# Splitting the last matmul tile of an attention-and-MLP kernel into two column halves, and storing two early tiles together

## The chip, the cores and the metric

The kernel runs on one core of a Trainium2 chip. A core has five engines with instruction streams of their own: TensorE (PE in the profile; its weight loads are listed as PEld), VectorE (DVE), ScalarE (ACT), GpSimd (POOL) and SyncE (SP), which here only issues transfers. Transfers are moved by 16 DMA engines. Data lives in SBUF (128 partitions); matmul results land in PSUM, which has banks of 512 fp32 columns per partition. The metric is the device time of one execution, in microseconds; lower is better.

## What is computed

```python
def attn(x, state):            # x [8,8,512,64], state [8,8,32,64], fp32
    scale = 1.0 / np.sqrt(64)
    a  = softmax(scale * x @ state^T)      # each token reads the state
    xread = a @ state
    a2 = softmax(scale * state @ x^T)      # the state reads the tokens
    sread = a2 @ x
    return concatenate([xread, sread], axis=2)      # 512 + 32 rows per batch

def reference(x, state, moe_w_in, moe_w_out):
    t = attn(x, state)                     # [8,8,544,64]
    t = t.transpose(0, 2, 1, 3).reshape(8 * 544, 512)
    h = t @ moe_w_in                       # [4352, 2048]
    return maximum(0.01 * h, h) @ moe_w_out  # [4352, 512] fp32
```

## The kernel before

The work is done batch by batch, b = 0 to 7, and the order of every engine's instructions is written out by hand. For one batch, `a_scores` makes the scores, the softmaxes run on DVE and ACT, and `a_m` folds the state into the first weight matrix (M = state times w_in), so that `ff1` makes one 128-row slice of the hidden layer from the softmax alone: 16 slices per batch, each evicted by ACT (L447) with the leaky ReLU. The second product (hidden layer times w_out, 512 token rows by 512 columns per batch) is spread between the slices of the next batch.

For batches 0 and 1 the second product is plain: `piece(b, hT, i, jq)` adds four of the sixteen contraction steps of the token tile i (0 to 3), with matmuls of 512 columns (L547). `y_store` (L554) copies the finished PSUM tile into SBUF and issues its store on SP (L558); tiles 2 and 3 of batch 0 are kept in one PSUM tile of two banks, `pyw`, and copied by ACT and DVE.

From batch 2 on the second product uses a scheme with seven block products in place of eight. `product(b, n, v)` (L615) makes product n for the half v of the rows: eight matmuls of 256 columns (L642) that add into PSUM "x" (n = 1, 6, 7, 4) or "b" (n = 2, 5, 3). Between them `keep` copies a partial sum away, and `y_add` adds a kept sum while evicting. For the last batch, 7, PSUM "x" is made of two separate places (`ppw`), one for each half v. Product 4 is the last to be added; what stands in "x" after it is the output block.

The order of the end is: a loop over c = 0, 1 that makes the hidden layer for all state rows (`f_product`, L520, matmuls of 128 columns) with batch 7's products 2, 5, 6 and 7 in between; the second product of the state rows (`two_product`, L699, `ppr`), whose results leave in eight stores (L1285), four on SP's queue and four on ACT's; product 3 of batch 7 with its eviction by DVE (L739) and its store (L745); and product 4:

```python
    for v in range(2):
        product(b, 4, v)
        (VEC, SCA)[v](y_block(b, 1, 0)[:, v], prods[b]["x"][v])
        nc.sync.dma_start(rows_of(b)[2 + v][:, :HN], y_block(b, 1, 0)[:, v])
```

`VEC` and `SCA` are copies on DVE and ACT. HN is 256.

At the start PE has little to do until the first inputs are in. `spin(p, n, w)` (L161) issues n matmuls of w columns on zeros, whose results nobody reads; they stand between the transposes `x0_t` (L784) and the scores `scores0` (L800) of batch 0's heads, and DVE takes maxima from the scores (`max0`, L830).

A buffer of a pool is written again when its last readers are done. Transfers that SP and ACT issue carry one of eight completion counters in turn, and a transfer waits for the one that used its counter before.

Of the kernel before, what the change touches and what calls it, by code (L numbers as in the profile page):

```python
# [9 lines left out]
P = 128  # L10
B, H, S, D = 8, 8, 512, 64
NS = 32
DFF = 2048
DM = 512
# [6 lines left out]
FP32 = mybir.dt.float32  # L21
AF = mybir.ActivationFunctionType
ALU = mybir.AluOpType
# [4 lines left out]
def kernel(  # L28
# [9 lines left out]
    nc = tc.nc  # L38

    consts = ctx.enter_context(tc.tile_pool(name="consts", bufs=1))  # L40
# [5 lines left out]
    ypool = ctx.enter_context(tc.tile_pool(name="ypool", bufs=3))  # L46
    psum = ctx.enter_context(tc.tile_pool(name="psum", bufs=2, space=bass.MemoryType.PSUM))
# [5 lines left out]
    VEC, SCA, POO = nc.vector.tensor_copy, nc.scalar.copy, nc.gpsimd.tensor_copy  # L53
# [104 lines left out]
    def spin_bank():  # L158
        return psum.tile([P, S], FP32, name="pspin", tag="py")

    def spin(p, n, w=S):  # L161
        for _ in range(n):
            nc.tensor.matmul(p[:, :w], lhsT=idle[:, :P], rhs=idle[:, :w], start=True, stop=True)
# [375 lines left out]
    ys = {}  # L539
# [12 lines left out]
            y_store(b, i, copy)  # L552

    def y_store(b, i, copy):  # L554
        tag = ("ysb", "s1", "ysb", "s6")[i]
        ysb = ypool.tile([P, DM], FP32, name="ysb", tag=tag, bufs=3 if tag == "ysb" else 1)
        copy(ysb[:], ys[b, i].py)
        nc.sync.dma_start(rows_of(b)[i], ysb[:])  # L558

    HN = DM // 2  # L560
    HJ = 8
# [12 lines left out]
    def w_block(r, c, j0, j1):  # L574
        return w_out_bf[:, HJ * r + j0:HJ * r + j1, HN * c:HN * (c + 1)]
# [12 lines left out]
    hTs, sums, prods = {}, {}, {}  # L588
# [20 lines left out]
    def w_of(n, j):  # L609
        if n < 4:  # L610
            r, c = {1: (0, 0), 2: (1, 0), 3: (1, 1)}[n]
            return w_block(r, c, j, j + 1)[:, 0]
        return tw[{4: 4, 5: 1, 6: 2, 7: 3}[n]][j // 4][:, j % 4]

    def product(b, n, v, j0=0, j1=8):  # L615
        q = prods.setdefault(b, {})
        bank = "x" if n in (1, 6, 7, 4) else "b"
        first = n in (1, 2, 5) and v == 0 and j0 == 0
        if first:
            if b == B - 1 and n == 1:  # L620
                ts = [psum.tile([P, 2, DM], FP32, name="ppw", tag=t, bufs=1) for t in ("sc", "big")]
                q[bank] = [t[:, 0, :HN] for t in ts]
                q["whole", bank] = None
            else:
                t = psum.tile([P, 2, HN], FP32, name=f"pp{bank}", tag="py")
                q[bank] = [t[:, u] for u in range(2)]
                q["whole", bank] = t[:]
        wide = b == B - 1 and n == 1
        q["open", bank] = first or (wide and j0 == 0)
        at = slice(P * v, P * (v + 1))  # L630
        low = slice(HN * 1 + P * v, HN * 1 + P * (v + 1))
        for j in range(j0, j1):
            lhsT = {
                1: lambda: hTs[b][:, j, at],
                2: lambda: hTs[b][:, HJ + j, at],
                4: lambda: hTs[b][:, HJ + j, low],
                3: lambda: sums[b, 4][:, j, at],
                5: lambda: sums[b, 1][:, j, at],
                6: lambda: sums[b, 2][:, j, at],
                7: lambda: sums[b, 3][:, j, at],  # L640
            }[n]()
            nc.tensor.matmul(  # L642
                q[bank][v], lhsT=lhsT, rhs=w_of(n, j), start=q["open", bank] and j == 0,
                stop=j == 7, skip_group_check=True,
            )

# [71 lines left out]
    def keep(b, n):  # L718
        q = prods[b]
        if n == 5:  # L720
            t = consts.tile([P, 2, HN], FP32, name="s5", tag="stf4")
        else:
            t = ypool.tile([P, 2, HN], FP32, name=f"s{n}", tag=f"s{n}", bufs=1)
        q[n] = t
        for to, of in bank_parts(q, "b" if n == 5 else "x", t[:]):
            SCA(to, of)

    def y_block(b, u, c):
        q = prods[b]
        if ("y", u) not in q:  # L730
            q["y", u] = ypool.tile([P, 2, DM], FP32, name="ysb", tag="ysb")
        return q["y", u][:, :, HN * c:HN * (c + 1)]

    def y_add(b, u, c, bank, n):
        q = prods[b]
        kept = q[n][:]
        for v, (to, of) in enumerate(bank_parts(q, bank, y_block(b, u, c))):
            in1 = kept if q["whole", bank] is not None else kept[:, v]
            nc.vector.tensor_tensor(out=to, in0=of, in1=in1, op=ALU.add)  # L739

    def pair_rows(b, u):
        return out[b * SROW:b * SROW + S, :].rearrange("(p t) f -> p t f", t=NT)[:, 2 * u:2 * u + 2]
# [7 lines left out]
    def after(b, n):  # L750
        if n == 1:
            keep(b, 1)
        elif n == 2:
            y_add(b, 0, 0, "b", 1)
        elif n == 6:
            keep(b, 6)
        elif n == 5:
            keep(b, 5)
        elif n == 7:
            y_add(b, 1, 1, "x", 5)  # L760
        elif n == 3:
            y_add(b, 0, 1, "b", 6)
            y_pair(b, 0)
        elif n == 4:
            SCA(y_block(b, 1, 0), prods[b]["whole", "x"])
            y_pair(b, 1)

    def rows_of(b):
        return out[b * SROW:b * SROW + S, :].rearrange("(p t) f -> t p f", t=NT)
# [119 lines left out]
    for q in range(2):  # L889
        cast_x0(q, VEC)  # L890
        x0_t(q)
        if q == 0:
            st1_evict()
            bank = spin_bank()
            spin(bank, 3, S // 2)
    spin(bank, 2, S // 2)
    scores0(0)
    cast_x0(2, VEC)
    x0_t(2)
    spin(bank, 2, S // 2)  # L900
    scores0(1)
    cast_x0(3, VEC)
    x0_t(3)
    bank = spin_bank()
# [3 lines left out]
    scores0(2)  # L908
    max0(2)
    rows0(0)  # L910
    spin(bank, 2, S // 2)
    scores0(3)
    max0(3)
    spread0(scn[0], m, False)
# [5 lines left out]
    q = [recip0(0)]  # L920
# [145 lines left out]
    for s in range(16):  # L1066
        ff1(a1, h1, s)
        if s in (1, 3):
            two = ((2, SCA), (3, VEC)) if s == 1 else ((0, SCA), (1, SCA))
            for i, copy in two:  # L1070
                piece(0, h0, i, 3, copy=None, js=half[1])
            for i, copy in two:
                y_store(0, i, copy)
        elif s % 2:
            piece(*fill[s // 2 - 2])
        if s == 4:
            a_scores(a2)
            pm = a_m(a1, 3, "big")
            a_max(a2)
            a_diff_halves(a2)  # L1080
            a_max2(a2)
        elif s == 5:
            m_evict(a1, 3, pm, SCA)
            load_state(1)
        elif s == 7:
            a_exp_half(a2, 0)
            a_open(att_of[3], 3)
            a_xt_dma(att_of[3])
        elif s in (9, 11):
            if s == 9:  # L1090
                a_exp_half(a2, 1)
            a_exp2(a2, s // 2 - 4)
            if s == 9:
                a_a2t_pair(0, (0,))
                a_recip(a2)
                a_probs(a2)
            else:
                a_probs2(a2)
                load_x(4, nc.sync)
        elif s == 13:  # L1100
            a_probs2(a1)
            a_a2t_pair(0, (1,))
            pm = [a_m(a2, 0, "big"), a_m(a2, 1, "sc")]
            m_evict(a2, 0, pm[0], SCA)
            m_evict(a2, 1, pm[1], VEC)
            q1 = two_open(h1, 2 * P, ("S0", "S1"), "py")
            for n in (1, 2, 3):
                two_sum(q1, n, 0, 4, nc.vector)
            two_sum(q1, 3, 4, 8, nc.vector)
# [19 lines left out]
    for b in range(2, B):  # L1129
# [22 lines left out]
        for s in range(16):  # L1152
# [75 lines left out]
            if b == 7 and s in FA_AT:  # L1228
                i = FA_AT.index(s)
# [23 lines left out]
    b = B - 1  # L1253
    for c in range(2):
        f = f_open(c)
        for n, own in (
            (1, ()), (2, ((2, 5)[c], 0)), (6, ()), (5, ((2, 5)[c], 1)),
            (7, ()), (3, ((6, 7)[c], 0)), (4, ((6, 7)[c], 1)),
        ):
            f_product(f, n)  # L1260
            if own:
                product(b, *own)
                if own[1]:
                    after(b, own[0])
            if c == 0 and n == 2:
                for m in (1, 2):
                    s_sum(b, m, 4, 8, nc.vector)
                for j in range(0, HJ, 2):
                    s_sum(b, 4, j, j + 2, nc.gpsimd)
        if c == 0:  # L1270
            y_pair(b, 0, 0, HN)
            q = two_open(hs, 0, None, "ph")
            for n in range(1, 5):
                two_sum(q, n, 0, 4, nc.vector)
# [14 lines left out]
        product(b, 3, v)  # L1289
    y_add(b, 0, 1, "b", 6)  # L1290
    y_pair(b, 0, HN, DM)
    for v in range(2):
        product(b, 4, v)
        (VEC, SCA)[v](y_block(b, 1, 0)[:, v], prods[b]["x"][v])
        nc.sync.dma_start(rows_of(b)[2 + v][:, :HN], y_block(b, 1, 0)[:, v])


# [28 lines left out]
```

## Time and profile before

| | us |
|---|---|
| median of three runs | 202.05 (201.94 to 202.19) |
| the profiled execution | 202.76 |
| its span | 201.0 |
| PE busy within the span | 195.4 (97%) |
| last matmul ends | 197.80 |
| last copy, on ACT (L1294) | 197.84 to 198.21 |
| last store issued on SP (L1295) | from 198.22 |
| last packets seen | 199.6 |

The profile lists, for the profiled execution, what each engine did and when. A line of the timeline has the start, the duration, the engine, the line of the kernel, the operation with its output and input, the shapes and the number of merged instructions; what stands in brackets is the idle time before it and what ended it. Matmuls are pipelined, so the duration of one (273 ns for 256 columns) is longer than the distance from one to the next; the distance is read from a block, its time divided by the number. SPq and ACTq are the issuing of transfers on the queues of SP and ACT, not the moving of the bytes; the time from issue to landing is given by line.

### The profile page before, as it was taken

How to read it: one execution, taken by the hardware profiler on the slowest of the kernel's cores; microseconds unless marked ns; L12 is line 12 of the kernel's file. 1: busy time of each engine (PE TensorE's matmuls, PEld its weight loads, DVE VectorE, ACT ScalarE, POOL GpSimd, SP SyncE). 2: the span in 40 equal slices, each digit the busy share in tenths (PEclk: the TensorE clock that was granted, in tenths of full speed). 3: DMA queues.
4: the chain of work that ended last, by engine and by line, in shares of the span. 5: the costliest groups of instructions: out<-in, count | busy, mean ns of one | idle time of the engine just before them, and what ended most of it. 6: DMA issues, size and time to landing. Idle time of an engine off the chain costs nothing.

```text
span 201.0 us, 4628 instructions
## 1 busy us (share of the span) xinstructions
PE 195.4 (97%) x1880; PEld 130.1 (65%) x1880; DVE 158.7 (79%) x241; ACT 141.9 (71%) x274; POOL 72.6 (36%) x76
## 2 busy tenths in 40 slices
PE   7998999999999999999999999999999999999993
PEld 3643534443476767776776677676767777799982
DVE  3665799399999989985999889898999945984712
ACT  3678738899889868766887779777868555757420
POOL 8823272992091373037300760054004600540000
PEclk9999999999999999999999999999999999999999
DMA  6999998697999944852473404220025302210115
GB/s 198 207 207 297 212 290 147 119 346 170 196 219 228 308 49 72 237 216 55 88 225 139 128 16 92 104 109 0 0 104 157 58 0 104 108 49 8 52 38 170
DMA packets 38773, 27.75 MB, mean 138 GB/s; under 512 B 24416, under 2 KB 35808, under 8 KB 38752
## 3 DMA queue, kind: packets, MB, share of 16 engines
q1 hardware_dynamic: 33584, 20.78, 39.3%
q0 software_dynamic: 4832, 6.29, 15.4%
q10 hardware_dynamic: 336, 0.39, 0.8%
q8 instruction: 14, 0.23, 0.5%
q14 instruction: 7, 0.06, 0.1%
HBM read 17.30 MB, written 8.91 MB: 130 GB/s over the span
## 4 chain that ended last, share of the span: by engine, by line
PE 91%; DMA 3%; DVE 2%; ACT 1%; ACTq 1%; SPq 0%; issue 0%
PE ph L442 24%; PE ppx L642 18%; PE ppb L642 15%; PE py L547 7%; PE ppr L699 6%; PE pm L421 4%; PE pyw L547 3%; PE pf L520 3%; PE ppw L642 3%; DMA xf<-in_x_dram 2%; PE psr L394 2%; PE php L947 1%; PE ph L947 1%; PE sc L256 1%; DMA out_dram<-ysb 1%; DVE m L830 1%
## 5 line engine op out<-in xcount | busy, mean ns | idle before, releaser
L447 ACT ACTIVATE hT<-ph 128x512 bf16<-128x512 f32 x112 | 66.7, 605 | 25.2 <-PE ph L442 24.5
L442 PE MATMUL ph<-aT,M 128*128 128x512 bf16 x224 | 65.5, 380 | 0.0
L607 POOL TENSOR_TENSOR S<-hT,S 128x512 bf16<-128x512 bf16 x24 | 32.1, 1357 | 82.2 <-DVE S L607 55.5
L642 PEld LDWEIGHTS <-S 128*128 128x128 bf16 x384 | 37.0, 98 | 12.7 <-issue 0.9
L642 PEld LDWEIGHTS <-hT 128*128 128x128 bf16 x288 | 28.0, 98 | 11.1
L607 DVE TENSOR_TENSOR S<-hT 128x1024 bf16<-128x1024 bf16 x24 | 25.0, 1069 | 3.3 <-ACT hT L447 3.3
L442 PEld LDWEIGHTS <-M 128*128 128x128 bf16 x224 | 20.9, 98 | 8.8 <-issue 2.9
L642 PE MATMUL ppx<-tw,S 128*128 128x256 bf16 x160 | 20.8, 273 | 0.0
L547 PEld LDWEIGHTS <-hT 128*128 128x128 bf16 x96 | 9.1, 98 | 11.4 <-issue 1.0
L547 PE MATMUL py<-w_out_bf,hT 128*128 128x512 bf16 x64 | 16.0, 380 | 0.0
L739 DVE TENSOR_TENSOR ysb<-ppb,s 128x512 f32<-128x512 f32 x12 | 8.3, 692 | 6.2 <-PE ppb L642 6.1
L642 PE MATMUL ppb<-tw,S 128*128 128x256 bf16 x96 | 12.4, 273 | 0.0
L642 PE MATMUL ppb<-w_out_bf,hT 128*128 128x256 bf16 x96 | 12.4, 273 | 0.0
L642 PE MATMUL ppb<-w_out_bf,S 128*128 128x256 bf16 x96 | 12.3, 273 | 0.0
L435 ACT CAST M<-pm 128x1024 bf16<-128x1024 f32 x11 | 11.2, 1018 | 0.3 <-PE pm L421 0.3
L642 PE MATMUL ppx<-w_out_bf,hT 128*128 128x256 bf16 x80 | 11.2, 273 | 0.0
L347 ACT ACTIVATE e<-sc,mcol 128x512 bf16<-128x512 f32 x16 | 11.1, 700 | 0.0
L586 POOL TENSOR_TENSOR tw<-w_out_bf 128x512 bf16<-128x512 bf16 x8 | 9.0, 1153 | 4.2 <-DMA w_out_bf<-in_moe_w_out_dram 4.2
L642 PE MATMUL ppx<-tw,hT 128*128 128x256 bf16 x80 | 10.4, 273 | 0.0
L341 DVE TENSOR_REDUCE mcol<-sc 128x2 f32<-128x1024 f32 x8 | 9.7, 1214 | 0.0
L266 DVE TRANSPOSE_TENSOR_REDUCE mrow<-sc 128x32 f32<-128x1024 f32 x7 | 8.7, 1242 | 1.2 <-PE sc L256 1.2
L132 POOL CAST xb<-xl 128x2048 bf16<-128x2048 f32 x5 | 9.5, 1892 | 0.0
(148 smaller groups left out, 322.5 us busy)
## 6 DMA issues: line engine op xcount, KB each, us to landing
out_dram<-ysb SPq DMA_DIRECT2D x11, 512.0 KB, 2.6
xl<-in_x_dram SPq DMA_DIRECT2D x5, 1024.0 KB, 6.4
out_dram<-ysb SPq DMA_DIRECT2D x9, 256.0 KB, 4.7
w_in_bf<-in_moe_w_in_dram POOLq DMA_DIRECT2D x4, 512.0 KB, 9.8
xf<-in_x_dram SPq DMA_DIRECT2D x4, 256.0 KB, 3.7
w_out_bf<-in_moe_w_out_dram POOLq DMA_DIRECT2D x4, 256.0 KB, 13.6
x<-in_x_dram POOLq DMA_DIRECT2D x2, 512.0 KB, 14.6
w_out_bf<-in_moe_w_out_dram POOLq DMA_DIRECT2D x2, 512.0 KB, 16.5
```

Source lines behind the costliest of these rows:

```text
L132: nc.gpsimd.tensor_copy(xt[b][:].rearrange("p t h d -> p h t d"), xl[b][:].rearrange("p h (t d) -> p h t d", t=NT),)
L266: nc.vector.tensor_reduce(out=m1[:], in_=flat.rearrange("p (c j) -> p c j", j=NS), axis=AX.X, op=ALU.max, apply_transpose=True,)
L341: nc.vector.tensor_reduce(out=a.m2[:], in_=a.sc[:], axis=AX.X, op=ALU.max, negate=True)
L347: nc.scalar.activation(out=a.e2[:, g], in_=a.sc[:, g, :], func=AF.Exp, bias=a.m2[:, g:g + 1], accum_out=a.r2[:, g:g + 1],)
L435: copy(a.M[:, :, cols], pm[:])
L442: nc.tensor.matmul(ph[:], lhsT=a.M[:, g, P * j:P * (j + 1)], rhs=a.aT[:, g, :], start=(g == 0), stop=(g == 1),)
L447: nc.scalar.activation(out=hT[:, j, :], in_=ph[:], func=AF.Prelu, scale=1 / SCALE, alpha=0.01)
L547: nc.tensor.matmul(y.py, lhsT=hT[:, j, P * i:P * (i + 1)], rhs=w_out_bf[:, j, :], start=(j == 0), stop=(j == 15),)
L586: eng.tensor_tensor(out=tw[n][u][:, at], in0=in0, in1=in1, op=ALU.subtract)
L607: eng.tensor_tensor(out=part(n), in0=in0, in1=in1, op=op)
L642: nc.tensor.matmul(q[bank][v], lhsT=lhsT, rhs=w_of(n, j), start=q["open", bank] and j == 0, stop=j == 7, skip_group_check=True,)
L699: nc.tensor.matmul(q.bank[w], lhsT=lhsT, rhs=w_of(n, j), start=n in (1, 2, 5) and j == 0, stop=j == HJ - 1, skip_group_check=True,)
```

## The change

1. Product 4 of batch 7 is made in other pieces. The half v = 0 stays as it was. The half v = 1 is made in two column halves of 128: the first adds into "x" as before, is copied by ACT and stored through ACT's queue. The second does not add into "x" but starts in a PSUM bank of its own, `end`. What "x" held for these columns before product 4 has been copied to SBUF earlier, by ACT, right after product 7 (`last`). DVE adds `end` and `last`, and SP stores the result.
2. Tiles 2 and 3 of batch 0 are copied into one SBUF buffer of 1024 columns and leave in one store of 4 KB rows, in place of two stores of 2 KB rows.
3. The idle matmuls between the first transposes and scores keep their number of columns, but are issued as 512 columns in place of two times 256.

```diff
+    def y_store_pair(b, copies):
+        ysb = ypool.tile([P, 2, DM], FP32, name="ysb", tag="ysb")
+        for v, copy in enumerate(copies):
+            copy(ysb[:, v], ys[b, 2 + v].py)
+        nc.sync.dma_start(pair_rows(b, 1), ysb[:])
...
-    def product(b, n, v, j0=0, j1=8):
+    def product(b, n, v, j0=0, j1=8, c0=0, c1=HN, bank_of=None):
...
             nc.tensor.matmul(
-                q[bank][v], lhsT=lhsT, rhs=w_of(n, j), start=q["open", bank] and j == 0,
+                q[bank][v][:, c0:c1] if bank_of is None else bank_of,
+                lhsT=lhsT, rhs=w_of(n, j)[:, c0:c1],
+                start=(q["open", bank] or bank_of is not None) and j == 0,
                 stop=j == 7, skip_group_check=True,
             )
...
             bank = spin_bank()
-            spin(bank, 3, S // 2)
-    spin(bank, 2, S // 2)
+            spin(bank, 1)
+            spin(bank, 1, S // 2)
+    spin(bank, 1)
     scores0(0)
...
-    spin(bank, 2, S // 2)
+    spin(bank, 1)
     scores0(1)
...
-    spin(bank, 2, S // 2)
+    spin(bank, 1)
     scores0(3)
...
-            for i, copy in two:
-                y_store(0, i, copy)
+            if s == 1:
+                y_store_pair(0, (SCA, VEC))
+            else:
+                for i, copy in two:
+                    y_store(0, i, copy)
...
+                if own == (7, 1):
+                    last = consts.tile([P, P], FP32, name="last", tag="stf2")
+                    SCA(last[:], prods[b]["x"][1][:, P:])
...
-    for v in range(2):
-        product(b, 4, v)
-        (VEC, SCA)[v](y_block(b, 1, 0)[:, v], prods[b]["x"][v])
-        nc.sync.dma_start(rows_of(b)[2 + v][:, :HN], y_block(b, 1, 0)[:, v])
+    y = y_block(b, 1, 0)
+    product(b, 4, 0)
+    VEC(y[:, 0], prods[b]["x"][0])
+    nc.sync.dma_start(rows_of(b)[2][:, :HN], y[:, 0])
+    end = psum.tile([P, P], FP32, name="end", tag="ph")
+    product(b, 4, 1, c1=P)
+    SCA(y[:, 1, :P], prods[b]["x"][1][:, :P])
+    nc.scalar.dma_start(rows_of(b)[3][:, :P], y[:, 1, :P])
+    product(b, 4, 1, c0=P, bank_of=end[:])
+    nc.vector.tensor_tensor(out=y[:, 1, P:], in0=end[:], in1=last[:], op=ALU.add)
+    nc.sync.dma_start(rows_of(b)[3][:, P:HN], y[:, 1, P:])
```

More of the change, by code (lines that the diff above doesn't have):

```diff
@@ L554, in y_store @@
     def y_store(b, i, copy):
-        tag = ("ysb", "s1", "ysb", "s6")[i]
+        tag = ("ysb", "s1")[i]
         ysb = ypool.tile([P, DM], FP32, name="ysb", tag=tag, bufs=3 if tag == "ysb" else 1)
```

## The prediction

> **What bounds the kernel now.** I read the page first, then the timeline of the last 10 us, then the chain of waits and the timeline of the first 14 us, then the waits between 36 and 62 us. All times are of the one profiled execution, counted from the start of its span.
>
> ```profile
> span 201.0 us, 4628 instructions
> ...
> PE 195.4 (97%) x1880; PEld 130.1 (65%) x1880; DVE 158.7 (79%) x241; ACT 141.9 (71%) x274; POOL 72.6 (36%) x76
> ...
> PEclk9999999999999999999999999999999999999999
> ...
> PE 91%; DMA 3%; DVE 2%; ACT 1%; ACTq 1%; SPq 0%; issue 0%
> ```
>
> TensorE (PE) is the bound at 97% busy, with its clock granted in full. Only three things can move the time: PE's own work, the first 14 us, in which PE waits for others, and what comes after its last matmul. The timeline of the end shows the last part:
>
> ```profile
> 195.89 1.91 PE L642 MATMUL ppw<-tw,hT 128*128 128x256 bf16 x16
> ...
> 196.81 0.39 SPq L745 DMA_DIRECT2D out_dram<-ysb  x1
> 196.96 0.42 DVE L1294 COPY ysb<-ppw 128x256 f32<-128x256 f32 x1 [0.18 <-PE ppw L642]
> 197.41 1.16 SPq L1295 DMA_DIRECT2D out_dram<-ysb  x2
> 197.84 0.37 ACT L1294 COPY ysb<-ppw 128x256 f32<-128x256 f32 x1 [3.12 <-DMA out_dram<-ysb]
> ```
>
> The columns are start, duration, engine and line. PE ends at 195.89 + 1.91 = 197.80. ACT copies the last tile from 197.84 to 198.21, and SP issues its store at 198.22 (two issues in 197.41 to 198.57, the second 0.35 long). The copy's named releaser, an earlier store, is not the true one: the copy starts 0.04 after PE's end, as the DVE copy starts 0.04 after PE's end of the other tile. The DMA line of L1295 gives 1.8 us from issue to landing for the shortest of the two stores; the last, with nothing ahead of it, is the 1.8, so it lands near 200.02, and 0.98 us of closing waits follow. The chain is therefore: last matmul, 0.41 for copy and wait, 1.8 for the store, 0.98.
>
> The moves of that store are in the stretch 199 to 201 us, which holds nothing else:
>
> ```profile
> DMA packets 144, 0.13 MB, mean 66 GB/s; under 512 B 16, under 2 KB 144, under 8 KB 144
> ...
> q1 hardware_dynamic: 144, 0.13, 18.9%
> ```
>
> 128 rows of 1 KB and 16 tiny completions. 18.9% of 2.0 us on 16 engines is 6.05 us; over the 128 rows that is at most 47 ns for a row, and each engine moves 8 of them one after the other, 0.38 us.
>
> **Part 1, the last tile in halves.** *Matmuls.* Eight of 128x256 become sixteen of 128x128, each with its own weight load. The chain has eight of the first kind in 0.87 (109 ns each), and for the second kind it has the blocks of L520:
>
> ```profile
> 184.23 0.87 PE ppb L642 x8
> 185.10 0.89 PE pf L520 x16
> 186.00 0.87 PE ppw L642 x8
> ```
>
> Sixteen in 0.89, 56 ns each, with sixteen weight loads of 98 ns lying beside them. So the tile costs 0.89 instead of 0.87: **+0.02**. It starts at 195.89 + 8 x 0.109 = 196.76; its first half is done at 196.76 + 7 x 0.056 + 0.219 (the duration of one L520 matmul) = 197.37, its second at 197.82.
> [...]
>
> *First half.* ACT copies 128x128 from 197.41; L191, the same size, took 0.27. Its store goes out on ACT's own queue at 197.70, not behind SP's. Packets began 0.83 (last store) to 0.89 (L745's) after an issue, so from about 198.55. The pair's and tile 2's stores keep the engines at 0.94 busy until 198.85; another 64 KB at their 340 GB/s is 0.19, so all is out by 199.05. It lies beside the second half.
>
> *Second half.* It goes to a bank of its own, so PE writes it while ACT reads the old bank. DVE then adds the kept part, 128x128: L739 takes 692 ns for 512 columns and 424 for 256, so 134 less again for 128, 0.29, against ACT's 0.37: **-0.08**. DVE is free (its copy of tile 2 ends at 197.38). Adding is needed because the kept partial stays in the other bank; it costs no more than a copy there. SP's issue comes at 198.16.
>
> *The last store* is half as large: 128 rows of 512 B, still eight per engine. No row of 512 B is in the trace. Upper end: 47 ns as now, no gain. Lower end: the stretch 46 to 48 us moves 805 packets, 803 of them under 512 B (256 B), in 42.3% of 2.0 us on 16 engines, 17 ns each: 8 x 30 = 0.24 gained. On the line between the two, 512 B takes 27 ns: 8 x 20 = **-0.16**. I take that, since a 2 KB to 1 KB step of landings points the same way: 64 KB stores land in 1.6 at the least, the 128 KB one in 1.8. Its packets start at 198.16 + 0.83 = 198.99, with at most 0.06 of the first half still ahead.
>
> *The kept part.* ACT's new copy of 128x128 (0.27) comes after L726/L496. ACT idles 1.00 us ahead of L704 (188.10 to 189.10); the copy waits for DVE's add from the same bank (188.23 + 0.42 = 188.65), so it ends at 188.94. Without that cover L704 would be up to 0.27 late, and its reader on DVE starts at 190.03, 0.56 after it: nothing. Cost 0.
>
> **Part 2, batch 0's tiles 2 and 3 in one store.** SP loses one of the four L558 issues (0.35 to 0.90). The store now waits for DVE's copy (38.06 to 38.75) instead of ACT's (to 38.03): tile 2 leaves 0.67 later. Behind it on SP stand the stores of tiles 0 and 1, which wait for ACT's copies (ends 39.48, 39.99) and are issued from 39.52: no later than now. Then come the eight state loads from 40.87, and a transpose issued at 47.20 that lands 4.3 later, at 51.5, for matmuls at 52.87: 1.4 of cover. SP's transfers wait for the eighth before them to land; one fewer only loosens this. Between 36 and 62 us the view of waits gives PE's weight loads one wait for a DMA, 0.4 us for the transposed state at 39.49, of which PE itself idles about 0.1. So 0, with -0.1 as the far end; a loss would need more than the 1.4.
>
> **Part 3, the idle matmuls of the start** (not in the short title, but in the diff): nine of 256 columns become four of 512 and one of 256, the same 2304 columns in the same places. At 109 ns and 215 (L547, four in 0.86) that is 0.98 against 0.97. One pair lies on the chain:
>
> ```profile
> 6.42 0.40 PE pxth L784 x4
> 6.82 0.22 PE pspin L163 x2
> 7.04 0.13 PE sct L800 x4
> ...
> 7.19 0.77 DVE m L830 x2
> ```
>
> 0.22 stays 0.22. A weight load that is now gone might have held PE for up to its 98 ns, but DVE is busy with L139 until 7.07, so -0.1 is the most; a loss has no source, as neither columns nor order change. Taken as 0.
>
> **Sum.** +0.02 - 0.08 - 0.16 = **-0.22 us**, all in the tail. The profiled execution took 202.76 around a span of 201.0 (1.76 outside it): it should become 200.8 and 202.5. The three timed runs have their median at 202.05, 0.71 below the profiled one; I carry the difference over: 201.83, say **201.85**.
>
> **Rivals.**
> 1. *The store does not shrink*: rows cost by number, not bytes. For it: no 512 B row is seen. Against: 47 ns and 17 ns at 1 KB and 256 B. Then only +0.02 - 0.08 = -0.06: 202.0. [...]
> 2. *Slower: weight loads become the bound* of the halved tile. PEld rows have 98 ns each, and sixteen in a row make 1.57 instead of 0.89: +0.68 on -0.22 gives 202.5. It decides from a pitch of 70 ns on (56 + 0.22/16), and exceeds 0.2% from 95. Against it stands L520 in seven places with 0.89. [...]
> 3. *The fresh bank is not free in time*, so the split doesn't do what it says: the compiled order has the second half's first matmul wait for DVE. If that means the add at 193.47 to 193.90, which empties the bank, it is long past; if tile 2's copy (to 197.38), PE stalls from 197.21 to 197.42 and +0.21 cancels all: 202.05. A first-half store that runs into the last one's packets for its whole 0.19 gives the same.
> 4. *More*: the two far ends of -0.1 in parts 2 and 3 come as well: -0.42, 201.6.
>
> **How the numbers follow.** Forecast 0.62, rival 1 0.15, rival 2 0.05, rival 3 0.08, rival 4 0.10. About 0.2% (0.40 us) is what a measurement of this kernel can tell from no change; the three runs lie within 0.25. Below 201.65 are rival 4 and the forecast's edge (512 B rows near the 256 B price): 0.15. Above 202.45 is rival 2 and a little for the unknown: 0.07. The rest, 0.78, is within. The range runs from 201.5 (the lower end of the row price with both far ends, -0.5) to 202.25 (rival 3, and half of rival 2's way).
>
> **What would show it.** Right: sixteen matmuls of the last tile in about 0.89; the final DVE add near 0.29, starting 0.04 after PE; the last store's rows at 24 to 30 ns and a landing near 1.6; the time from PE's end to the end of the span 0.24 shorter (it is 3.2). Wrong: a gap between the two halves on PE, rows that stay at 45 ns, a last landing that belongs to ACT's queue, or a difference that already stands at 188 us, before the tail.

## The result, and the profile after

The changed kernel is slower: 203.11 us median (202.99 to 203.35, six runs) against 202.24 (201.94 to 202.64, six runs of the kernel before beside it), a ratio of 1.0045 with a 95% interval of 1.0032 to 1.0058. Forecast were 201.85 and a range of 201.5 to 202.25. Medians here are over all runs of a kernel, ratios over those within 1.5% of its fastest; `e2_spin` below, with two slower runs of twelve, has 202.92 as its median without them.

The page of the changed kernel, the lines that answer to those of before:

```profile
span 201.3 us, 4609 instructions
...
PE 194.0 (96%) x1856; PEld 130.1 (65%) x1884; DVE 158.6 (79%) x242; ACT 142.1 (71%) x275; POOL 72.6 (36%) x76
...
PEclk9999999999999999999999999999999999999999
...
q8 instruction: 14, 0.23, 0.5%
...
PE 78%; DMA 15%; POOL 3%; issue 1%; SPq 1%; ACT 1%; DVE 0%; POOLq 0%
```

The clock is granted in full as before (1.0 in both profiled executions). The chain that ended last was 91% PE and 3% DMA; now it is 78% and 15%. Somewhere PE waits for a transfer, and from there back the chain runs through transfers and no longer through PE. Where it comes over to PE shows in its steps between 35 and 41 us (start, duration, what):

```profile
35.34 4.49 DMA st_t<-stb
...
39.88 0.41 PE sc L256 x8
```

The chain goes through the transposed state `st_t`, which a transpose on SP's queue (L214) makes for the scores of a later batch. The waits of PE between 36 and 62 us, with their total, number and longest:

```profile
PE sc L256 <- DMA st_t<-stb: 0.7, 1, 0.7
```

Before, PE had no wait in this stretch: `st_t` landed at 39.03, and the first matmul that reads it ran at 39.50. Now it lands at 39.83, and PE is idle for 0.66 until 39.88. Compared instruction by instruction, the changed kernel is 0.35 us ahead at 36 us (in the profiled execution of before, the head waited longer for a weight transfer, which is a matter of that execution); from the scores at L256 on it is 0.38 behind, and stays there up to the tail. So 0.73 us are lost at this one place, and the difference stands long before the tail.

The tail of the changed kernel, its timeline:

```profile
196.27 1.48 PE L648 MATMUL ppw<-tw,hT 128*128 128x256 bf16 x16
...
197.59 0.61 PE L648 MATMUL end<-tw,hT 128*128 128x128 bf16 x8
197.79 0.27 ACT L1313 COPY ysb<-ppw 128x128 f32<-128x128 f32 x1 [2.69 <-DMA out_dram<-ysb]
...
198.08 0.36 ACTq L1314 DMA_DIRECT2D out_dram<-ysb  x1
198.24 0.29 DVE L1316 TENSOR_TENSOR ysb<-end,last 128x128 f32<-128x128 f32 x1 [0.47 <-PE end L648]
198.56 0.34 SPq L1317 DMA_DIRECT2D out_dram<-ysb  x1
```

This tail is built as forecast: no gap between the halves on PE, ACT's copy 0.27, DVE's add 0.29 and 0.04 after PE's end. From PE's end (198.20) to the last issue are 0.36, before 0.43. But from the last issue to the end of the span it takes 2.74, where it took 2.75: the store landed 1.82 after its issue, before 1.84. The tail gained 0.07 in all.

A third part lies outside the span. Time less span was 1.79 to 1.80 (medians) in the runs of the kernel before, in every group of experiments; in the six runs of the changed kernel it was 1.77 to 2.12, 2.0 in the mean. So of 0.9 us, 0.7 are in the span and 0.2 behind it.

### The profile page after: what moved, and what is told of

Its sections match the earlier page's. It is cut to its first block, busy times and chain, and to the rows that moved or that the text cites. A ratio compares the mean times of both kernels' runs of the same rounds, so it can differ in the third digit from the quotient of the medians.

```text
span 201.3 us, 4609 instructions
## 1 busy us (share of the span) xinstructions
PE 194.0 (96%) x1856; PEld 130.1 (65%) x1884; DVE 158.6 (79%) x242; ACT 142.1 (71%) x275; POOL 72.6 (36%) x76
## 4 chain that ended last, share of the span: by engine, by line
PE 78%; DMA 15%; POOL 3%; issue 1%; SPq 1%; ACT 1%; DVE 0%; POOLq 0%
PE ph L442 21%; PE ppx L648 18%; PE ppb L648 16%; DMA xl<-in_x_dram 7%; DMA w_out_bf<-in_moe_w_out_dram 6%; PE ppr L707 6%; PE py L547 3%; PE pm L421 3%; PE ppw L648 3%; PE pf L520 3%; DMA st_t<-stb 2%; PE psr L394 2%; POOL w_in_bf L145 2%; PE sc L256 1%; SPq L240 1%
## 5 line engine op out<-in xcount | busy, mean ns | idle before, releaser
L442 PE MATMUL ph<-aT,M 128*128 128x512 bf16 x202 | 60.9, 379 | 0.1
```

What stands on the lines that cost most here:

```text
L442: nc.tensor.matmul(ph[:], lhsT=a.M[:, g, P * j:P * (j + 1)], rhs=a.aT[:, g, :], start=(g == 0), stop=(g == 1),)
```

## The experiments

All were timed in five rounds against the kernel before, which gave 202.19 to 202.41 beside them. "TensorE instructions" counts matmuls and weight loads, and one branch at each end: 3762 before (1880 of each kind on its page), 3770 in the changed kernel (1884 of each; its page lacks the records of 28 matmuls).

### The parts alone

`e1_tail` has only the split tile, `e2_spin` only the wider idle matmuls, `e3_pair` only the paired store, `e4_spin_pair` the last two together; each is the kernel before with these parts of the diff above.

> The split last tile alone, without the pair store and with the idle matmuls as before. Theory A (the loss lies in the middle: PE idles 0.66 us at 39.88 for the transposed state, which landed 4.5 us after its issue in place of 2.9, and the tail itself gained 0.07, from a shift of +0.38 before it to +0.31 at the end of the span): this kernel has neither the pair store nor other idle matmuls, so 0.0 to -0.1 us against before. Theory B (the loss lies outside the span: the time is 2.0 us above the span in place of 1.76, because the last store of a second queue has to be closed): +0.3 or more, with the span itself equal or shorter. Theory C (the idle matmuls of the start): 0.0 to -0.1.

> The idle matmuls in 512 columns alone. Theory C: the whole +0.9 or most of it appears here, as a shift within the first 14 us. Theories A and B: within 0.1 us of before; in the changed kernel the shift against before was +0.13 at 6.9 us and -0.35 by 36 us, so nothing that lasts.

> The pair store of batch 0 alone. Theory A, if the pair store is what delays the transposed state: +0.4 to +0.9 us, with PE idle ahead of the first scores from the transposed state (L256) for 0.5 us or more. If the late landing at 39.88 was chance of one execution: within 0.1 of before. Theories B and C: within 0.1.

> The change without the split last tile. Theory B: within 0.1 us of before, all of the +0.9 being the tail's. Theory A: +0.4 to +0.9 as the pair store alone. Theory C: the whole +0.9. If the parts simply add up, this is the sum of the two kernels with one part each.

| kernel | median us | ratio to before [95%] |
|---|---|---|
| e1_tail | 203.31 | 1.0057 [1.0037, 1.0078] |
| e2_spin | 203.00 | 1.0033 [1.0018, 1.0048] |
| e3_pair | 202.28 | 1.0010 [0.9997, 1.0024] |
| e4_spin_pair | 203.13 | 1.0045 [1.0028, 1.0063] |

The paired store costs nothing that can be told from zero. The wider idle matmuls cost nearly all of what the whole change costs. The split tile alone costs more than the whole change, so the parts don't add. The theories that put the loss outside the span, or into the wide matmuls of the head, don't fit these four: time less span is 1.8 in all of them, and the loss of `e2_spin` is not in the first 14 us, where the wide matmuls are, but at `st_t`, for which its PE is idle for 0.64 us.

What these runs share shows in the transfers by queue. The transfers of `e2_spin` between 34.8 and 37.2 us (packets, MB, share of 16 engines):

```profile
DMA  0000979999998999900000000000010001000100
...
DMA packets 523, 0.16 MB, mean 66 GB/s; under 512 B 521, under 2 KB 521, under 8 KB 521
...
q14 instruction: 1, 0.01, 4.7%
q8 instruction: 1, 0.02, 3.7%
```

and of the kernel before in the same stretch:

```profile
DMA  0300999999980000000379999999999999999999
...
DMA packets 1532, 0.38 MB, mean 159 GB/s; under 512 B 1532, under 2 KB 1532, under 8 KB 1532
```

The q8 packet is 16 KB of a stream of instructions (the page's q8 row has 14 such packets, 0.23 MB). 3.7% of 2.4 us on 16 engines is 1.4 us: the packet took that long. The kernel before has the same packet, its third, at 33.2 us; here it comes at 35.1 us, beside the transpose of the state, and a third as many packets pass in the same stretch. The rows that begin with DMA give the busy share of the 16 engines in 40 slices of 0.06 us, in tenths: in `e2_spin` the transfers do not slow down but nearly stop at 35.8 us, 0.7 us into the fetch, for the rest of the stretch. SP's timeline shows the transpose itself, of the changed kernel:

```profile
35.34 2.44 SPq L214 DMA_TRANSPOSE st_t<-stb  x1
```

and of the kernel before:

```profile
36.10 1.19 SPq L214 DMA_TRANSPOSE st_t<-stb  x1
```

Its issue takes 2.44 instead of 1.19, it lands 4.5 after its start instead of 2.9, and PE waits. That gave the next theory, F: the four matmuls and four weight loads that the wider form saves shift the point at which the next block of TensorE's instructions is fetched. And `e1_tail`, with 16 instructions more, has a packet that the kernel before has not. Its page, and its timeline of the end:

```profile
q8 instruction: 15, 0.25, 0.5%
```

```profile
196.65 1.04 SPq L1300 DMA_DIRECT2D out_dram<-ysb  x1
...
197.78 0.40 SPq L1307 DMA_DIRECT2D out_dram<-ysb  x1
```

The fifteenth block is fetched at 195.81 for 1.49 us. The issue of tile 2's half store takes 1.04 instead of 0.36, ACT's 0.73 instead of 0.36, the last store goes out 0.40 after its add has ended (197.38), and lands after 2.14 instead of 1.8.

### Is it the count, or what was changed?

`e5_wide_count` keeps the wide matmuls and gives the count back; `e6_drop4` takes the count without a wide matmul; `e7_plus8` adds 16 instructions at the start and leaves the tail alone; `e8_cand28` has the split tile and the paired store with 58 instructions more than before.

```diff
 e5: -spin(bank, 2, S // 2)              (three places, and one of the 3)
     +spin(bank, 1)
     +spin(bank, 1, NS)                  # NS = 32 columns
 e6: -spin(bank, 3 or 2, S // 2)         (four places)
     +spin(bank, 2 or 1, S // 2)
 e7: -spin(spin_bank(), 7)
     +spin(bank, 5); spin(bank, 2, S // 2); spin(bank, 8, S // 16)
 e8: -spin(spin_bank(), 7)               (beside the parts 1 and 2)
     +spin(spin_bank(), 28, S // 4)
```

> The widened idle matmuls of the change, and four idle matmuls of 32 columns beside them, so that TensorE issues as many instructions as in the kernel before; the rest is the kernel before. Theory F (the cost of the spin edit is that eight fewer TensorE instructions move the third 16 KB block of its instruction stream from about 33 us to about 35.4 us, into the transpose of the state st_t): the block is fetched at 32.3 to 33.3 us as before, the issue of st_t on SP's queue takes 1.2 us and not 2.1 to 2.4, and the time is that of the kernel before, 202.1 to 202.4. Theory W (wide idle matmuls themselves cost, through the clock or by delaying the real work behind them): the time stays with that of the spin edit alone, 202.9 to 203.1, with st_t untouched.

> Four of the nine idle matmuls of 256 columns are left out and none is widened: eight fewer TensorE instructions (four matmuls, four weight loads), as with the spin edit, with less TensorE work and no wide matmul. The output is unchanged. Theory F: the third block is fetched at about 35.4 us, the issue of st_t takes over 2 us, and the time is 202.8 to 203.2. Theory W: no loss, 201.9 to 202.4, as no matmul is wider.

> Eight more idle matmuls with their weight loads in the first group of idle matmuls (seven of 512 columns become five of 512, two of 256 and eight of 32: nearly the same columns), and the tail as before. TensorE then issues 16 instructions more, as many as with the split tail alone. Theory F: a fifteenth block is fetched at about 195.8 us, it holds up the issue of the last transfers as in the run of the tail alone, and the time is 202.7 to 203.4 though the tail's work is untouched; the third block is fetched about 1 us earlier than 33 us. Theory T (the split itself, its halves, its small stores or the add, is what cost the tail run its time): the time is that of the kernel before, 202.1 to 202.5.

> The split tail and the paired store, the narrow idle matmuls of the kernel before, and the first group's seven idle matmuls of 512 columns as 28 of 128: 42 instructions more on TensorE, and 58 more than the kernel before. Theory F: the fifteenth block is fetched some 2 to 3 us earlier than 195.8, ahead of the last transfers, and the third block before 32 us, clear of st_t: the tail's split shows its own gain, 201.8 to 202.4. Theory T or W: the split tail costs as in the run of the tail alone, 203.0 to 203.5.

| kernel | third block at, us | issue of st_t, us | blocks | median us | ratio [95%] |
|---|---|---|---|---|---|
| e5_wide_count | 32.69 | 1.19 | 14 | 202.24 | 1.0000 [0.9989, 1.0010] |
| e6_drop4 | 34.77 | 2.39 | 14 | 202.79 | 1.0022 [1.0009, 1.0035] |
| e7_plus8 | 32.47 | 1.19 | 15 | 203.07 | 1.0040 [1.0024, 1.0056] |
| e8_cand28 | 32.16 | 1.19 | 15 | 202.57 | 1.0025 [1.0007, 1.0042] |

`e5_wide_count` decides against the wide matmuls as the cause: all of them are there and the loss is gone. `e6_drop4` has less work and no wide matmul, and the loss is there. (Two of its twelve runs stand at 201.96 and 202.00, without the loss, as does one of `e2_spin`, 201.95; no trace of these runs shows what the block did in them.) Its timeline:

```profile
34.82 2.39 SPq L214 DMA_TRANSPOSE st_t<-stb  x1
...
39.31 0.41 PE L256 MATMUL sc<-xT,st_t 64*32 64x512 bf16 x8 [0.55 <-DMA st_t<-stb]
```

`e7_plus8` leaves the tail's code as it was and adds eight idle matmuls 190 us earlier. Its TensorE is about 0.5 us ahead of the profiled execution of before from 25 us to its end (197.31 beside 197.80); the span then ends 0.49 behind. From its timeline:

```profile
194.25 3.34 ACTq L1288 DMA_DIRECT2D out_dram<-ysb  x4
...
196.32 0.76 SPq L745 DMA_DIRECT2D out_dram<-ysb  x1
```

The same issues take 1.84 and 0.39 before. As only TensorE's instructions were changed and q8 has 15 packets in place of 14, this run also shows that q8 carries TensorE's. The expectation for `e8_cand28` was a miss: its fifteenth block, at 193.67, is not early enough. The stores of L1299 take 3.14 on SP and 2.45 on ACT, and the last store lands 2.54 after its issue. So a block at 193.67 goes with longer issues of stores, as the one at 195.81 in `e1_tail` does.

In the kernel before, PE has no wait between 36 and 62 us, though a block is fetched at 57.4; but where a block lies beside the transpose and PE waits for `st_t`, it is idle: for 0.55 us in `e6_drop4`, 0.66 in the changed kernel, 0.82 in `e15_drop9` and 1.16 in `e13_after_no1`.

### Versions in between

`e10_tail_2`, `e11_tail_4` and `e12_tail_6` are the change with one, two and three pairs of idle matmuls widened instead of four, so with 3776, 3774 and 3772 TensorE instructions.

```diff
       (the diff of the change, but for these)
 e10:  spin(bank, 2, S // 2)              (kept narrow in three of four places)
 e11:  spin(bank, 2, S // 2)              (kept in two)
 e12:  spin(bank, 2, S // 2)              (kept in one)
```

> The change with one pair of idle matmuls widened instead of four: two TensorE instructions fewer early instead of eight, 14 more in all than the kernel before. Theory F (what counts is where the 16 KB blocks of TensorE's instruction stream fall): the third block near 33 to 33.5 us, in front of the transpose of st_t, whose issue takes 1.2 us; whether the fifteenth block is fetched at the end is open (six instructions under the run of the tail alone, which has it, and six above the changed kernel, which has not): with it 202.8 to 203.4, without it 201.9 to 202.3.

> The change with two pairs of idle matmuls widened instead of four: four TensorE instructions fewer early, 12 more in all than the kernel before. Theory F: the third block between 33 and 35.4 us; if the issue of st_t stays at 1.2 us and no fifteenth block is fetched, 201.9 to 202.3; with either of the two, 202.7 to 203.4.

> The change with three pairs of idle matmuls widened instead of four: six TensorE instructions fewer early, 10 more in all than the kernel before, two more than the changed kernel. Theory F: no fifteenth block; the third block near 35 us; if the issue of st_t takes over 2 us, 202.7 to 203.1; if it stays at 1.2 us, 201.9 to 202.3.

| kernel | third block at, us | issue of st_t, us | time less span, us | median us | ratio [95%] |
|---|---|---|---|---|---|
| e10_tail_2 | 32.93 | 1.19 | 1.75 to 2.89 | 203.02 | 1.0024 [1.0004, 1.0043] |
| e11_tail_4 | 35.07 | 2.17 | 1.73 to 2.52 | 203.12 | 1.0046 [1.0024, 1.0069] |
| e12_tail_6 | 36.42 | 3.05 | 1.73 to 2.08 | 202.74 | 1.0026 [1.0008, 1.0044] |

The third block does what was expected, though in `e12_tail_6` it comes at 36.4 and not near 35. The fifteenth does something that was not: it comes behind the span. The transfers of `e10_tail_2` between 200 and 204 us, with its span of 200.6:

```profile
q8 instruction: 1, 0.02, 1.4%
```

The block is fetched at 202.24, and this run took 2.28 more than its span. The same packet is in the traces of `e11_tail_4` and, with the changed kernel's own 3770 instructions, of `e14_after_sp1`, at 202.1 and 202.5. In the trace of the changed kernel itself I see none, though that run took 2.05 more than its span; what is shown is only that a time less span of over 2.1 us appears at these counts, in part of the runs of five of the six kernels with 3770 to 3776 (not of `e12_tail_6`, which reaches 2.08), and in no run at 3762 or less, nor at 3778 and above. That the fetch is its cause is not shown.

### Where the store's gain went

`e9_half_store` is the kernel before with the second half of the last store left out (those values of the output are not written). `e13_after_no1` is the changed kernel without the store of the first half (likewise), `e14_after_sp1` has that store on SP's queue.

```diff
 e9:  -nc.sync.dma_start(rows_of(b)[3][:, :HN], y_block(b, 1, 0)[:, 1])
      +nc.sync.dma_start(rows_of(b)[3][:, :P], y_block(b, 1, 0)[:, 1, :P])
 e13: -nc.scalar.dma_start(rows_of(b)[3][:, :P], y[:, 1, :P])
 e14: -nc.scalar.dma_start(rows_of(b)[3][:, :P], y[:, 1, :P])
      +nc.sync.dma_start(rows_of(b)[3][:, :P], y[:, 1, :P])
```

> The kernel before, with the second half (128 columns) of the very last store left out, so its 128 rows are 512 B and not 1 KB; those output columns are not written. Theory P (the prediction's price: 8 rows per DMA engine at 27 ns and not 47 ns): the end comes 0.16 us sooner, 202.0 to 202.1 beside 202.24. Theory G (the last rows land at the same time whatever their size, since what lies between the issue and the end is not the moving of these bytes, as the changed kernel's 2.74 us from last issue to the span's end beside 2.78 suggests): under 0.08 us, 202.2 to 202.3.

> The changed kernel without the store of the first half of the last tile (128 x 128 values of the output are not written). Theory Q (this store, just ahead of the last one and on another queue, is what eats the gain of the small rows): the last store lands about 1.63 us after its issue instead of 1.82, and the time falls by 0.15 to 0.25 us from that of the changed kernel, to 202.85 to 203.0. Theory R (the gain of small rows is lost elsewhere): landing 1.8 us, time 203.05 to 203.2.

> The changed kernel with the store of the last tile's first half on SP's queue instead of ACT's. Theory Q with two queues as the cause (packets of two queues alternate on an engine): landing of the last store 1.65 to 1.72 us, 202.9 to 203.05. If the bytes ahead are the cause, and not the second queue: landing 1.8 us, 203.05 to 203.2; a little more if the issue on SP (0.36 us) is in the way of the last one.

Times: 202.01 (0.9984 [0.9968, 0.9999]), 203.32 (1.0052 [1.0036, 1.0069]) and 203.08 (1.0044 [1.0030, 1.0058]). The landing of the last store, from its issue, is 1.82 in the changed kernel and 1.68 in `e14_after_sp1`. In `e9_half_store` it is the minimum of its line (which has two stores), and in `e13_after_no1` it has a line of its own:

```profile
DMA to landing us min/median/max: 1.6/1.9/2.2
```

```profile
DMA to landing us min/median/max: 1.6/1.6/1.6
```

In `e9_half_store` and `e13_after_no1` a last store of 512 B rows lands 0.21 sooner (1.63 against 1.84), as the prediction had it, but with a second store just ahead on another queue, in the changed kernel, the 0.2 are gone (1.82). They are not lost among the rows. From its issue to the end of its last packet the store takes 1.37 in the kernel before, 1.20 in `e13_after_no1` and still 1.25 in the changed kernel, though its packets (199.44 to 199.81) overlap with those of the first half (199.21 to 199.59); that packets of two queues alternate on one engine is not shown, only that between 199.44 and 199.59 packets of both begin. From there to the landing it takes 0.47, 0.43 and 0.57. The landing is the last of sixteen counter updates (for the last store of the changed kernel from 200.22 to 200.38), and in the changed kernel those of the last three stores follow one another almost without a break from 199.86 to 200.38; whether they hold one another up is not shown. On SP's queue (`e14_after_sp1`) 1.68 remains of the 1.82, but the issue of the last one moves 0.17 back behind it (0.94 after tile 2's issue instead of 0.76 to 0.77), so nothing is won. The time of `e13_after_no1` was a miss, over all expected values. Its third block fell at 37.24, the transpose landed 4.4 after its start, PE was idle for 1.16 at `st_t`, and its time less span ran up to 2.76; so its time doesn't measure the store, and only its landing does.

### The split tile without displaced blocks

`e15_drop9` is the kernel before without its nine idle matmuls of 256 columns; `e16_drop9_tail` has the split tile as well.

```diff
-            spin(bank, 3, S // 2)
-    spin(bank, 2, S // 2)                 (three places)
```

> The kernel before without its nine idle matmuls of 256 columns: 18 TensorE instructions fewer, none widened. Theory F: the third block moves further than with eight fewer (35.4 us), to 36.5 us or later, behind the issue of the state's transpose (1.2 us again), and the time is that of the kernel before, 202.0 to 202.5; if the block still falls between 34 and 36.5 us, 202.7 to 203.2. If the idle matmuls are needed to hold the clock, the granted clock near 14 to 18 us falls and the time rises by over 0.5 us without a stall at st_t.

> The split tail of the change on the kernel without the nine idle matmuls of 256 columns: two TensorE instructions fewer than the kernel before, so no fifteenth block. Theory F: beside e15_drop9 it shows the split tail alone, 0.03 to 0.12 us faster than that run (the 0.04 to 0.10 of the traces), with no stall at the end. If the split has a cost of its own outside these blocks, it is slower than e15_drop9 by over 0.3 us.

202.87 (1.0027 [1.0012, 1.0043]) and 203.49 (1.0062 [1.0050, 1.0074]). The pair failed as a test: the third block fell at 35.03 and 37.00, and the transpose's issue took 2.31 and 1.92; PE was idle at `st_t` for 0.82 in the one and not at all in the other. The granted clock stayed full without the idle matmuls (1.0 and 0.999 in the two profiled executions). So the pair was made again with the head untouched. `e17_skip8` leaves out eight matmuls of the last batch's product 2 (inner steps 1 to 4, both halves), `e18_skip8_tail` does so and has the split tile.

```diff
         for j in range(j0, j1):
+            if (b, n) == (B - 1, 2) and 1 <= j <= 4:
+                continue
```

> The kernel before, with eight matmuls and their eight weight loads of the last batch left out (inner steps 1 to 4 of product 2, both tiles; the output of that product's rows is so not the full sum): 16 TensorE instructions fewer, all of them after 100 us. Theory F: the head and the third block as before, st_t issue 1.2 us; up to 0.9 us faster than the kernel before (8 matmuls of 0.108 us), as these lie on TensorE's path. It serves as the base of the next run.

> The same with the split tail of the change: as many TensorE instructions as the kernel before, none of them moved ahead of 100 us. Theory F: no fifteenth block and no stall at st_t, so the split shows its own worth against e17_skip8: faster by 0.03 to 0.12 us, with 1.8 us from the last issue to its landing. Theory T (the split costs by itself): slower than e17_skip8 by 0.3 us or more.

202.34 (0.9997 [0.9979, 1.0014]) and 202.58 (1.0013 [0.9996, 1.0031]), 14 blocks each, the third at 32.7, the issue of `st_t` 1.18. The hoped-for 0.9 of the eight matmuls did not come; PE is 0.45 us earlier at 176 us than in `e5_wide_count` and has given half of it back by 178; why is open. The intervals of the two overlap, so the times alone do not rule out the gain of 0.03 to 0.12 that was expected; but the two profiled executions differ by 0.26 (202.28 and 202.02), and their traces show why. In `e17_skip8` the last store's issue (the second of L1297) and the closing instructions of SP (L1323):

```profile
L1297 SPq DMA_DIRECT2D out_dram<-ysb x2: 344/350/357, 196.7 to 197.5; - x2
DMA to landing us min/median/max: 1.8/2.0/2.2
```

```profile
L1323 SPq DRAIN  x3: 7/7/13, 199.4 to 199.7; - x3
```

and the same in `e18_skip8_tail`:

```profile
L1309 SPq DMA_DIRECT2D out_dram<-ysb x1: 345/345/345, 197.3 to 197.3; - x1
DMA to landing us min/median/max: 1.9/1.9/1.9
```

```profile
L1335 SPq DRAIN  x3: 7/7/13, 199.7 to 200.0; - x3
```

The store is issued and lands 0.2 earlier (199.15, before 199.32; PE came 0.14 earlier into this tail), and yet SP closes later. Between landing and closing lie 0.08 in the one and 0.51 in the other. At the end SP waits for the eight completion counters one after the other, about 0.06 us each where their transfers have landed (the first four in the kernel before at 198.69, 198.75, 198.82 and 198.88), and in the same order in these traces. In the traces the last store carries the eighth of this order in the kernel before and in the changed one, and the first in `e1_tail`, `e16_drop9_tail` and `e18_skip8_tail`.

With the eighth counter the last store is the last to be waited for. With the first, seven waits (0.43) stand behind it. The split tile's one more transfer moves the last one on to the first counter; the paired store takes one away, which puts it back on the eighth. In `e1_tail` and `e16_drop9_tail` the closing also comes 0.51 after the landing; in the six kernels with both parts and all stores it is 0.08. With the paired store alone (`e3_pair`) it is 0.14, one wait more.

In `e16_drop9_tail` there is one more thing that stays open: in its profiled execution weight transfers (`w_in`) came late at 12.8 and 16.5 us, which put it 1.25 us behind `e15_drop9`, and a change in the tail gives no reason for that.

## Why the prediction was wrong

**The step that failed is part 3**, the idle matmuls, "taken as 0", for "a loss has no source, as neither columns nor order change". It costs 0.7 us (`e2_spin`: 203.00 beside 202.26; with the count kept, `e5_wide_count`: 202.24 beside 202.26). Columns and order are indeed the same; what changed is the number of instructions, and with it the place of a 16 KB fetch. The trace of before had the signs: the q8 row on its page, the fetch at 33.2 us ahead of the transpose at 36.1, and only 0.46 us between the landing of `st_t` and its use. The prediction looked for cover at a later transpose (1.4 us) and passed this one over. Its reading of the 0.4 us at 39.49 as a wait for `st_t`, with 0.1 of it idle on PE, was wrong: the weight load starts 0.46 after the landing, PE is not idle there, and the same 0.42 stands in all eleven traces in which PE does not wait for `st_t`, whether it landed 0.07 or 0.85 us ahead.

**Part 2** was right: 0, and measured at a ratio of 1.0010 [0.9997, 1.0024]. The wait for the eighth transfer before, of which the forecast speaks, shows in the trace of before: the fourth of the state loads is issued at 43.88, and the input load issued at 37.35, eight transfers before it, landed at 43.87. What part 2 does to the counters at the end was not seen; without it the split tile would cost 0.43 more (0.51 from landing to closing in `e1_tail`, 0.08 in the changed kernel).

**Part 1, matmuls and add**: right in mechanism and size. No gap between the halves: PE writes `end` (197.59 to 198.20) while ACT reads `ppw` (197.79 to 198.06), so the stall on the bank (rival 3) did not come; from PE's end to the last issue 0.07 less, where -0.08 was forecast. Rival 2, weight loads as the bound, falls: from the start of `ppw`'s sixteen matmuls to that of `end`'s are 1.32 us in the timeline, which is eight of 256 columns at 0.109 and eight of 128 at 0.056, and no gap shows.

**Part 1, the last store, -0.16**: the price of the row was about right (e9: its 144 packets take 49.1% of 0.45 us on 16 engines, at most 28 ns for a row, where 27 was forecast, and the landing gains 0.21; that each engine moves eight of the 128 rows is the author's estimate), the sum was not. In the changed kernel the landing gains 0.02. The store of the first half, which was to lie "beside the second half", takes the rest: without it the landing is 1.63. Rival 3 had named that store, but by its packets running into the last one's; they do, for 0.05, and 0.14 come behind the last packet, which no part of the prediction had.

**The 1.76 outside the span, carried over**: it grew to 2.0 in the mean, and why is open.

Added up: 0.73 at `st_t`, -0.07 in the tail, 0.20 outside the span make 0.86; measured are 0.87. That this fits to 0.01 is luck, as the first two come from one execution of each kernel. Of what was to "show it", the clause "a difference that already stands at 188 us" applied.

How a fetch of one packet stretches the issue of a transpose to double its length is not shown: the trace does not tell which of the 16 engines a packet is on. That the two go together is: in the ten traces whose third block is fetched by 33.3 us the transpose's issue takes 1.18 to 1.19 us, and PE does not wait for `st_t`; in the ten with 34.7 or later it takes 1.9 to 3.1, but for `e13_after_no1`, where the landing is late instead, and PE waits in nine of them (not in `e16_drop9_tail`, whose scores come late themselves). The moment of the issue is not what matters: `e9_half_store` issues it at 35.33 and takes 1.19, the changed kernel at 35.34 and takes 2.44.

No kernel with the full output beat the one before; `e5_wide_count` equals it.

## What to carry to other kernels

Before pricing an edit at nothing because it changes no work, count the instructions it adds or takes on each engine: look up the instruction packets in the trace, see which transfers on the path stand next to one, and how few instructions would move it there. At the end of a kernel, see which completion counter the last transfer carries, since one transfer more put seven waits behind it here (0.43 us), and one less put one (0.06 us). A loss that doesn't add up over the parts of a change is a sign of such a displaced event, and a run that keeps the count while changing the work separates the two.

## What the runs showed of the hardware

- The fetch of a block of TensorE's instructions (16 KB) took 0.88 to 1.43 us in the traces of before and after and 1.49 in `e1_tail`. With one beside them the issue of a transpose took 1.9 to 3.1 (`e16_drop9_tail`, `e12_tail_6`) in place of 1.19, and that of a store 1.04 (`e1_tail`) in place of 0.36.
- Eight TensorE instructions fewer put the third fetch over 2 us later (32.7 in e5, 34.8 in e6, 35.1 in e2), more than the 0.9 us that four matmuls of 512 columns last; why so much is open.
- With 3770 to 3776 TensorE instructions part of the runs took up to 1.1 us more outside the span (2.89 beside 1.79); in three traces a block is fetched there (202.1 to 202.5).
- The closing waits on the completion counters took about 0.06 us each, and those behind the last landing counted: from it to SP's closing 0.08 us with none behind it (changed kernel), 0.51 with seven (`e18_skip8_tail`).
- Sixteen matmuls of 128 columns with a weight load each went at 56 ns apiece (L520, 0.89 us for sixteen), and a store with 512 B rows landed 0.21 us sooner than one with 1 KB rows (1.63 against 1.84), but not with a store on another queue just ahead of it (1.82).
